# Two heads' last attention rows scored in both halves of TensorE's columns, and ten more heads scored in split precision

## The chip, the cores and the metric

The kernel runs on one core of a Trainium2 chip. The metric is the device time of one execution in microseconds (us); of several runs the median counts. TensorE (PE in the rows) multiplies matrices and loads their weights (PEld), VectorE (DVE) and ScalarE (ACT) do elementwise work and read TensorE's results, GpSimd (POOL) does elementwise work on data in SBUF, and SyncE (SP) issues the DMA transfers. One thing is particular to this program: every engine works through its own list in order, so an instruction that waits holds back all that stand behind it on its engine.

## The reference, cut to what matters

Causal attention with a decay goes through two gated feed-forward layers. Four batches, eight heads, 576 positions, head width 64:

```python
scores = scale * np.matmul(q, k.transpose(0, 1, 3, 2))
log_f = np.log(np.clip(f, 0.0001, 1.0))
cum = np.cumsum(log_f, axis=-1)
decay = cum[:, :, :, None] - cum[:, :, None, :]
scores = np.where(causal, -1000000000.0, scores + decay)
attn = np.exp(scores - np.max(scores, axis=-1, keepdims=True))
attn = attn / (np.sum(attn, axis=-1, keepdims=True) + 1e-09)
attn_out = np.matmul(attn, v)
...
x = (x @ w_a) * (x @ w_b) @ w_out          # 2304 x 512, then 1536, then 512
...
g = rmsnorm(x) @ w_gate                     # the second layer, the same sizes
out = silu(g) * (rmsnorm(x) @ w_val) @ w_out2
```

## The kernel before, in words

The 2304 tokens are worked through in three chunks (640, 704 and 1024 wide), and each chunk goes through both layers in six phases. The products of the layers are made of a high and a low part of each operand: a `triple` is three matmuls (lines 903, 904, 905) in the type fp32r. These matmuls are nearly all of TensorE's work. The weights arrive as 64-bit numbers and are decoded in the first phase: the last step, on GpSimd, is the low part at line 764.

Attention is cut into jobs that are woven between the blocks of the layers. The list `ATT` says which: a batch, its blocks of 128 query rows (`ALL` is 0 to 128, 128 to 256, 256 to 384, 384 to 512 and the last one, 512 to 576, with 64 rows), and a number `sf`. Group 0 has the later rows of batch 0, group 1 batch 1 and the first 128 rows of batch 2, group 2 the rest of batch 2, group 3 batch 3. Heads are taken two at a time. A head below `sf` has its scores in plain fp32: one matmul of 66 contracted rows, which the trace shows as two records. The other heads are split: GpSimd copies (line 1890) and VectorE subtractions (line 1893) make high and low parts in `qa`, `ka` and `b` from the loaded `qk`, and a score is then two fp32r matmuls, one of 128 contracted rows from `qa` and `ka`, one of 68 from `b`. There is one buffer each of `qk` and `b`, and two each of `qa` and `ka`, which is one pair of heads.

`unit` (line 1922) scores one block of 128 rows of one head against all keys up to it. `packed` (line 1948) scores the last 64 rows of both heads of a pair in one tile of 128 partitions, in two column halves of 288 keys, each in an own bank `s` (there are two). It does so by first writing all 128 partitions with head 1, whose 128 query columns end at the last row, and then the lower 64 with head 0. After the softmax the probabilities are transposed (line 1565, fp32), copied out, and multiplied with the values (`values`, line 1978): fp32 matmuls with 64 weight columns, the two heads of a pair in turn, one to each half of the output's partitions. Where a group of other rows is light enough, the last 64 rows share this job with it, and stand ahead of it.

The order on each engine is made in advance by `Plan`: it knows a cost of every step and a priority, places the steps greedily, tries nine ways of weighing them for every stretch of 30 us, and writes the order out. A changed cost or an added step therefore moves instructions all over the program. `kind` marks TensorE steps in fp32, and a change from fp32 to fp32r counts 85 ns there.

Of the kernel before, what the change touches and what calls it, by code (L numbers as in the profile page):

```python
# [28 lines left out]
ALL = tuple((a, min(a + 128, S)) for a in range(0, S, 128))  # L29
FIRST = ((0, 128), (128, 256))  # L30
PE, ACT, DVE, POOL, SP = "PE", "ACT", "DVE", "POOL", "SP"
# [15 lines left out]

ATT = [
    (((0, ((256, 384), (384, 512), (512, 576)), 8),), ((0, 0.0, 0.22, 1.0),), 18000),
    (((1, ALL, 2), (2, ALL[:1], 8)), ((0, 0.22, 0.8, 1.0),), 5000),  # L50
    (((2, ALL[1:], 0),), ((1, 0.1, 1.0, 0.6), (2, 0.0, 0.2, 0.4)), 5000),
    (((3, ALL, 0),), ((2, 0.1, 1.0, 0.7), (3, 0.1, 0.88, 0.3)), 20000),
]
# [27 lines left out]
def mm(n):  # L81

    return max(107.0, 0.4375 * n + 7)


def values_cost(nkb, n):

    return nkb * 2 * (2 * n / 2.4 + 6) + 210
# [86 lines left out]
class Plan:  # L175
# [19 lines left out]
    def op(self, eng, cost, fn, reads=(), writes=(), prio=0.0, after=(), nbytes=0, start=0, port=False, kind=0):  # L195
        n = Node()
        n.port, n.kind = port, kind
        n.eng, n.cost, n.fn, n.prio, n.bytes, n.ready = eng, cost, fn, prio, nbytes, start
        deps, n.allocs, n.bufs, n.first = set(after), [], set(), set()
        for t in (*reads, *writes):  # L200
            b = t[0] if isinstance(t, tuple) and isinstance(t[0], Buf) else t
            if isinstance(b, Buf):
                if b.alloc is None:
                    b.alloc = n
                    n.allocs.append(b)
                    self.rings.setdefault(b.tag, []).append(b)
                elif b.alloc is not n:
                    n.first.add(b.alloc)
                if b not in n.bufs:
                    n.bufs.add(b)  # L210
                    b.users.append(n)
        for t in reads:
            assert t in self.writer, t
            deps.add(self.writer[t])
            self.readers.setdefault(t, []).append(n)
        for t in writes:
            if t in self.writer:
                deps.add(self.writer[t])
            deps.update(self.readers.get(t, ()))
            self.writer[t] = n  # L220
            self.readers[t] = []
        deps.discard(n)
        n.first -= deps
        deps |= n.first
        n.deps, n.outs, n.waiting = deps, [], len(deps)
        for d in deps:
            d.outs.append(n)
        n.given, n.att = (eng, cost, fn, start), False
        self.nodes.append(n)
        return n  # L230
# [153 lines left out]
class Kernel:  # L384
# [219 lines left out]
    def blocks(self, p):  # L604

        m, c = PHASES[p]
        n = range(len(CHUNKS[c][1]))
        if c == 0:
            if p:
                return [x for q in range(THIRDS) for x in self.plain_blocks(q, n)]  # L610
            ab = lambda fs, ss: [("ab", j, s) for f in fs for j in (2 * f, 2 * f + 1) for s in ss]
            y = lambda q, ss: [("y", i, q, s) for i in range(KT) for s in ss]
            cut = QF + ALONE
            return [
                *self.plain_blocks(0, [0]), *ab(range(QF, cut), [0]), *ab(range(cut, 2 * QF), n),
                *ab(range(QF, cut), [1]), *y(1, n), *self.plain_blocks(2, n), *self.plain_blocks(0, [1]),
            ]
        ahead = int(self.adjoins(p))
        out = [*((x, f) for f in range(2) for x in ("P1", "P2")), ("P7", 0)] if ahead else [("P1", 0), ("P7", 0), ("P2", 0)]
        for f in range(FT):  # L620
            out += [("P6", f), ("P4", f)]
            nxt = [[(x, f + 1)] if f + 1 < FT and (x == "P7" or f >= ahead) else [] for x in ("P1", "P7", "P2")]
            out += [*nxt[0], ("P5", f), *nxt[1], *nxt[2], ("P3", f)]
            if f == FT - 1 or (p < SWAP_AT and f % QF == QF - 1):
                out += [("y", i, f // QF, s) for i in range(KT) for s in n]
            elif p >= SWAP_AT and f and f % QF == FAST_AFTER:
                out += [("z", i, f // QF - 1, k) for k in range(len(FAST)) for i in range(KT // 2)]
        if self.adjoins(p + 1):
            out[-2 * KT :] = [("y", i, THIRDS - 1, s) for s in n for i in range(KT)]
        return out  # L630
# [1302 lines left out]
    def packed(self, c, u, tiles, t, sf):  # L1933

        nc, op = self.nc, self.op
        a, e = u
        r, w = e - a, e // 2
        assert 2 * r == 128
        s = [self.bank("s", S_BANKS) for _ in range(2)]
        qk = [x for y in tiles for x in y[1]]  # L1940
        for i in range(2):

            def scores(x, ks=slice(i * w, i * w + w)):

                for g in (1, 0):
                    n, y = g * r + r, tiles[g][0]
                    for j, (q, k) in enumerate(y):
                        nc.tensor.matmul(x[:n, :w], q.tile[:, e - n : e], k.tile[:, ks], start=j == 0, stop=j == len(y) - 1)  # L1948

            op(PE, 2 * (4 * w / 2.4 + 3 if sf else 2 * mm(w)), scores, reads=qk, writes=[s[i]], prio=t, kind=int(sf))  # L1950
        p = self.tile([128, S], "P", P_BUFS, pool=self.att)
        sm = self.tile([128, 2], "sm", 4, pool=self.att)
        self.exps(128, e, [self.mask[:, 0:w], self.mask_2], s, p, sm, 0, t + 600)
        self.norms(128, e, [p], sm, 2, t + 600)
        return p, None

    def values(self, c, hs, groups, tiles, t):

        nc, op = self.nc, self.op
        some = [self.moved(us, pss, t) for us, pss in groups]  # L1960
        reads = [x for r, _ in some for x in r]
        starts, width = [], 0
        for us, _ in groups:
            starts.append(width)
            width += us[-1][1] - us[0][0]
        blocks = lambda u: -(-u[1] // 128)
        rows = lambda u, i: min(128, u[1] - i * 128)
        pv = self.bank("tp", TP_BANKS)

        def product(x):  # L1970
            for (us, _), (_, at), start in zip(groups, some, starts):
                for j, u in enumerate(us):
                    o, n = start + u[0] - us[0][0], u[1] - u[0]
                    for i in range(blocks(u)):
                        k = rows(u, i)
                        for g in range(2):
                            y, to = at[g, j, i]
                            nc.tensor.matmul(  # L1978
                                x[64 * g : 64 * g + 64, o : o + n], tiles[g][2][0].tile[:k, i, :], y.tile[:k, to : to + n],
                                start=i == 0, stop=i == blocks(u) - 1,  # L1980
                            )

        op(
            PE, sum(values_cost(blocks(u), u[1] - u[0]) - 210 for us, _ in groups for u in us) + 210, product,
            reads=[*reads, *(x for y in tiles for x in y[2][1])], writes=[pv], prio=t + 5500, kind=1,
        )
        for (us, _), start in zip(groups, starts):
            self.valued(c, hs, us[0][0], us[-1][1], start, pv, t)
# [127 lines left out]
```

## Time and profile before

| what | us |
|---|---|
| median of 3 runs | 1075.48 |
| lowest and highest of them | 1072.12, 1080.87 |
| the profiled execution's own time | 1073.34 |
| its span, first to last instruction | 1071.3 |
| TensorE busy in it | 1050.6 |
| VectorE busy | 807.7 |
| ScalarE busy | 565.1 |
| GpSimd busy | 249.2 |

The time outside of the span is 2.0 us. A matmul's record covers its whole way through the array, and the next one starts before it ends; what one costs in a row of many is the distance from start to start. The chain of waits gives this distance, since it counts each piece up to where the next takes over.

### The profile page before, as it was taken

Reading aid. Unit: us, or ns where it says so; the run is one execution under the profiler, and the core shown is the slowest. Engines: PE = TensorE matmul, PEld = TensorE weight load, DVE = VectorE, ACT = ScalarE, POOL = GpSimd, SP = SyncE. Lnnn points to the kernel's source line nnn. Section 1 sums busy time; section 2 is a strip of 40 time slices with the busy share of each in tenths; the row PEclk is TensorE's granted clock in tenths of the full one; section 3 lists DMA queues with packets and bytes.
Section 4 is the critical chain, followed back from the end, with each engine's and each line's share of the span. In section 5 each row is a group of like instructions: output and inputs, shape, how many; then the busy total and the mean of one; then the engine's idle time right before and its main releaser. Section 6 shows DMA issues by size and latency. Waiting matters only on the chain.

```text
span 1071.3 us, 19068 instructions
## 1 busy us (share of the span) xinstructions
PE 1050.6 (98%) x6738; PEld 934.5 (87%) x6738; DVE 807.7 (75%) x1815; ACT 565.1 (53%) x1235; POOL 249.2 (23%) x254
## 2 busy tenths in 40 slices
PE   8999999999999999999999999999999999999998
PEld 6678889999999999999999999988888887788886
DVE  6787677779668877878779777765667469979974
ACT  6677578656444557665665663522333254444330
POOL 6423244312203134443541010000000023212000
PEclk9999999999999999999999999999999999999999
DMA  8989868989865986678789676786453634546332
GB/s 232 270 267 305 311 201 276 311 303 340 265 214 207 323 284 230 223 234 290 267 311 332 225 258 234 256 282 195 143 171 120 206 117 151 171 140 180 120 124 78
DMA packets 91707, 245.54 MB, mean 229 GB/s; under 512 B 13077, under 2 KB 23525, under 8 KB 91613
## 3 DMA queue, kind: packets, MB, share of 16 engines
q1 hardware_dynamic: 91612, 244.33, 68.7%
q8 instruction: 53, 0.87, 0.3%
q14 instruction: 42, 0.34, 0.1%
HBM read 163.27 MB, written 81.03 MB: 228 GB/s over the span
## 4 chain that ended last, share of the span: by engine, by line
PE 82%; DVE 8%; DMA 3%; issue 3%; POOL 2%; ACT 1%; SPq 0%; DVEq 0%; POOLq 0%; ACTq 0%
PE m L903 19%; PE m L905 18%; PE m L904 18%; PE tp L1978 4%; PE tp L1565 3%; PE s L1922 3%; PE s L904 2%; PE s L905 2%; PE s L903 2%; PE tp L904 2%; PE tp L905 2%; PE tp L903 2%; PE s L1948 2%; POOL w L764 1%; DMA w<-wd 1%
## 5 line engine op out<-in xcount | busy, mean ns | idle before, releaser
L903 PE MATMUL m<-E,w 128*128 128x512 f32 (+3 forms) x672 | 234.1, 348 | 4.9 <-ACT a L1291 1.7
L905 PE MATMUL m<-E,w 128*128 128x512 f32 (+3 forms) x672 | 227.4, 338 | 0.6 <-POOL w L764 0.6
L904 PE MATMUL m<-E,w 128*128 128x512 f32 (+3 forms) x624 | 212.7, 341 | 0.0
L1291 ACT ACTIVATE a<-m 128x352 f32<-128x352 f32 (+1 forms) x144 | 74.9, 526 | 146.6 <-PE m L905 146.1
L764 POOL TENSOR_TENSOR w<-w,w 128x512 fp32r<-128x512 f32 x72 | 98.4, 1372 | 201.9 <-ACT w L1614 149.9
L903 PEld LDWEIGHTS m<-E,w 128*128 128x128 f32 x672 | 126.7, 189 | 21.3 <-issue 3.7
L904 PE MATMUL m<-Eb,w 128*128 128x352 f32 (+3 forms) x432 | 140.9, 326 | 0.0
L905 PEld LDWEIGHTS m<-E,w 128*128 128x128 f32 x672 | 126.4, 188 | 11.4 <-POOL w L764 0.8
L1300 DVE TENSOR_TENSOR a<-m,a 128x352 f32<-128x352 f32 (+1 forms) x144 | 86.5, 602 | 58.6 <-PE m L905 57.7
L903 PE MATMUL m<-Eb,w 128*128 128x352 f32 (+3 forms) x384 | 127.5, 332 | 0.1
L904 PEld LDWEIGHTS m<-E,w 128*128 128x128 f32 x624 | 117.6, 189 | 11.1 <-issue 0.2
L905 PE MATMUL m<-Eb,w 128*128 128x352 f32 (+3 forms) x384 | 126.8, 330 | 0.0
L903 PE MATMUL m<-G,w 128*128 128x352 f32 (+2 forms) x352 | 111.0, 315 | 0.4 <-DVE xc L941 0.3
L905 PE MATMUL m<-G,w 128*128 128x352 f32 (+2 forms) x352 | 108.3, 308 | 0.2 <-POOL w L764 0.2
L904 PE MATMUL m<-G,w 128*128 128x352 f32 (+2 forms) x352 | 108.2, 307 | 0.0
L1524 ACT ACTIVATE P<-P,mn 128x512 f32<-128x512 f32 (+4 forms) x128 | 76.1, 596 | 23.6 <-DVE mn L1517 22.9
L904 PEld LDWEIGHTS m<-Eb,w 128*128 128x128 f32 x432 | 81.3, 188 | 4.3
L903 PEld LDWEIGHTS m<-Eb,w 128*128 128x128 f32 x384 | 72.2, 188 | 4.9 <-DVE a L1300 0.4
L905 PEld LDWEIGHTS m<-Eb,w 128*128 128x128 f32 x384 | 72.2, 188 | 4.3
L1427 ACT ACTIVATE G<-a 128x352 fp32r<-128x352 f32 (+3 forms) x100 | 47.1, 473 | 52.3 <-DVE a L1413 18.8
L1517 DVE CUSTOM_DVE_ANT_0 P<-s,mask 128x512 f32<-128x512 f32 (+4 forms) x128 | 61.5, 495 | 13.3 <-PE s L1922 7.0
L903 PEld LDWEIGHTS m<-G,w 128*128 128x128 f32 x352 | 66.3, 188 | 2.7 <-issue 1.2
(268 smaller groups left out, 2258.0 us busy)
## 6 DMA issues: line engine op xcount, KB each, us to landing
w<-wd SPq DMA_DIRECT2D x88, 512.0 KB
wd<-w SPq DMA_DIRECT2D x72, 512.0 KB
ws<-w SPq DMA_DIRECT2D x48, 512.0 KB
w<-ws SPq DMA_DIRECT2D x48, 512.0 KB
wf<-w SPq DMA_DIRECT2D x48, 256.0 KB
raw<-wo SPq DMA_DIRECT2D x24, 512.0 KB
w<-wf SPq DMA_DIRECT2D x48, 256.0 KB
w<-wd SPq DMA_DIRECT2D x48, 256.0 KB
```

Of the source, the lines that this page charges most:

```text
L764: nc.gpsimd.tensor_tensor(out=w.tile[:, :, 1, :], in0=i32.tile.bitcast(F32), in1=w.tile[:, :, 0, :].bitcast(F32), op=ALU.subtract)
L903: mm_(o, wh, xh, start=start, stop=False)
L904: mm_(o, wh, xl, start=False, stop=False)
L905: mm_(o, wl, xh, start=False, stop=stop)
L1291: nc.scalar.activation(z[:, :h], bank_.tile[:, :h], AF.Copy)
L1300: nc.vector.tensor_tensor(out=z, in0=bank_.tile[:, :h], in1=z, op=ALU.add)
L1427: nc.scalar.activation(out(0), x(), AF.Copy)
L1517: nc.vector.tensor_tensor_reduce(out=p.tile[:n, i * w : i * w + w], in0=s[i].tile[:n, :w], in1=masks[i][:n], scale=-0.125, scalar=mn.tile[ ...
L1524: nc.scalar.activation(o, o, AF.Exp, bias=mn.tile[:n, len(s) - 1 : len(s)], scale=-1.0, accum_out=sm.tile[:n, g : g + 1])
L1565: nc.tensor.transpose(ps.tile[:w, c : c + n], p.tile[:n, i * 128 : i * 128 + w], self.ident[:n, :n])
L1922: self.nc.tensor.matmul(x[:n, :e], q.tile[:, a:e], k.tile[:, :e], start=j == 0, stop=j == len(pairs) - 1)
L1978: nc.tensor.matmul(x[64 * g : 64 * g + 64, o : o + n], tiles[g][2][0].tile[:k, i, :], y.tile[:k, to : to + n], start=i == 0, stop=i == blo ...
```

## The change

Three things change. `ATT` asks for no fp32 scores in group 1 any more: the first two heads of batch 1 and the first rows of all eight heads of batch 2 become split. `packed` is written in two forms: for fp32 heads (batch 0 alone now) each head's 64 query columns go to their own half of the output partitions, head 0 and head 1 in turn; for split heads the two column halves of head 1 come first and then those of head 0, as four steps of the planner where there were two. `values` goes through its groups from the last to the first, so that the last 64 rows come last where they share the job.

```diff
-    (((1, ALL, 2), (2, ALL[:1], 8)), ((0, 0.22, 0.8, 1.0),), 5000),
+    (((1, ALL, 0), (2, ALL[:1], 0)), ((0, 0.22, 0.8, 1.0),), 5000),
...
-        for i in range(2):
-
-            def scores(x, ks=slice(i * w, i * w + w)):
-
-                for g in (1, 0):
-                    n, y = g * r + r, tiles[g][0]
-                    for j, (q, k) in enumerate(y):
-                        nc.tensor.matmul(x[:n, :w], q.tile[:, e - n : e], k.tile[:, ks], start=j == 0, stop=j == len(y) - 1)
-
-            op(PE, 2 * (4 * w / 2.4 + 3 if sf else 2 * mm(w)), scores, reads=qk, writes=[s[i]], prio=t, kind=int(sf))
+        pairs = [y[0] for y in tiles]
+
+        def scores(parts, *_):
+            for g, i, b, n in parts:
+                for j, (q, k) in enumerate(pairs[g]):
+                    nc.tensor.matmul(
+                        s[i].tile[b : b + n, :w], q.tile[:, e - n : e], k.tile[:, i * w : i * w + w], start=j == 0,
+                        stop=j == len(pairs[g]) - 1,
+                    )
+
+        if sf:
+            for i in range(2):
+                parts = [(g, i, g * r, r) for g in range(2)]
+                op(PE, 2.1 * w, partial(scores, parts), reads=qk, writes=[s[i]], prio=t + i, kind=1)
+        else:
+            for g in (1, 0):
+                for i in range(2):
+                    op(PE, 2 * mm(w), partial(scores, [(g, i, 0, r + g * r)]), reads=qk, writes=[s[i]], prio=t + 2 - 2 * g + i)
...
-            for (us, _), (_, at), start in zip(groups, some, starts):
+            for (us, _), (_, at), start in list(zip(groups, some, starts))[::-1]:
```

TensorE's list, the second pair of heads of batch 0, before: the packed fp32 scores (line 1948) into two banks, with the values of the pair before them (line 1978) in between.

```order
L1948 MATMUL s_726<-b_449 128x288
L1948 MATMUL s_726<-b_449 64x288
L1978 MATMUL tp_739<-pt_721,vr_434 64x64 x8
L1978 MATMUL tp_739<-pt_719,vr_434 64x64 x2
L1948 MATMUL s_758<-b_449 128x288
L1948 MATMUL s_758<-b_449 64x288
L1565 MATMUL tp_766<-ident,P_664 128x128 x3
```

And now (the packed scores are at line 1946, the values at line 1986):

```order
L1922 MATMUL s_706<-b_366 128x512
L1986 MATMUL tp_715<-pt_700,vr_434 64x64 x8
L1986 MATMUL tp_715<-pt_703,vr_434 64x64 x2
L1946 MATMUL s_738<-b_449 64x288 x2
L1946 MATMUL s_744<-b_449 64x288 x2
L903 MATMUL m_758<-E,w_678 128x256
```

No packed fp32 matmul has 128 output partitions any more, and the two banks follow each other.

TensorE's list, one values job of batch 1 in which the last 64 rows (output 64x64) share the tile with a block of 128 rows, before:

```order
L905 MATMUL m_2120<-G,w_2075 128x256
L1978 MATMUL tp_2143<-pt_2088,vr_1882 64x64 x8
L1978 MATMUL tp_2143<-pt_2091,vr_1882 64x64 x2
L1978 MATMUL tp_2143<-pt_2118,vr_1882 64x128
L1978 MATMUL tp_2143<-pt_2133,vr_1882 64x128
```

And the end of the same kind of job now:

```order
L1986 MATMUL tp_2183<-pt_2172,vr_1914 64x128
L1986 MATMUL tp_2183<-pt_2177,vr_1914 64x128
L1986 MATMUL tp_2183<-pt_2105,vr_1914 64x64 x8
L1986 MATMUL tp_2183<-pt_2119,vr_1914 64x64 x2
L1922 MATMUL s_2218<-ka_1912,qa_1863 128x512
```

The two rows of `x2`, whose matmuls contract over 64 positions, moved from the middle of the job to its end.

GpSimd's list, from the late part of group 0 on, before: the low parts of decoded weights (line 764) and between them the split copies of one pair of batch 1 (line 1890).

```order
L764 TENSOR_TENSOR w_1672<-w_1648,w_1672 128x2x256
L764 TENSOR_TENSOR w_1742<-w_1721,w_1742 128x2x256
L1890 TENSOR_SCALAR b_1771<-qk_599 64x576 x2
L764 TENSOR_TENSOR w_1838<-w_1797,w_1838 128x2x256
L764 TENSOR_TENSOR w_1891<-w_1853,w_1891 128x2x256
L764 TENSOR_TENSOR w_2075<-w_2045,w_2075 128x2x256
L1890 TENSOR_SCALAR qa_2135<-qk_1949 64x576
L1890 TENSOR_SCALAR ka_2141<-qk_1949 64x576
```

And now, over the same part of batch 1's first two pairs:

```order
L764 TENSOR_TENSOR w_1561<-w_1523,w_1561 128x2x256
L1890 TENSOR_SCALAR qa_1603<-qk_962 64x128
L1890 TENSOR_SCALAR ka_1605<-qk_962 64x128 x2
L1890 TENSOR_SCALAR qa_1624<-qk_962 64x128
L1890 TENSOR_SCALAR b_1622<-qk_962 64x128 x2
L1890 TENSOR_SCALAR ka_1629<-qk_962 64x128 x2
L1430 TENSOR_TENSOR G<-a_1538,G 128x256
L764 TENSOR_TENSOR w_1649<-w_1597,w_1649 128x2x256
L764 TENSOR_TENSOR w_1700<-w_1673,w_1700 128x2x256
L764 TENSOR_TENSOR w_1789<-w_1745,w_1789 128x2x256
L1890 TENSOR_SCALAR qa_1841<-qk_1725 64x576
L1890 TENSOR_SCALAR qa_1863<-qk_1725 64x576
```

A set of eight short copies for the first rows of batch 2 now stands between those of two pairs of batch 1, with weight parts behind it.

## Rows read from the trace of the kernel before

**Rows 1.** The page: busy time by engine, and TensorE's clock over 40 slices.

```profile
PE 1050.6 (98%) x6738; PEld 934.5 (87%) x6738; DVE 807.7 (75%) x1815; ACT 565.1 (53%) x1235; POOL 249.2 (23%) x254
...
PEclk9999999999999999999999999999999999999999
```

**Rows 2.** What TensorE waited for: total us, times, longest us.

```profile
PE tp L1565 <- ACT P L1548: 2.3, 4, 1.1
...
PE m L903 <- ACT a L1291: 1.7, 2, 1.0
...
PE m L905 <- POOL w L764: 0.8, 2, 0.6
```

**Rows 3.** Busy time by stretch: length, then each engine's.

```profile
core 0: us, PE busy (x) PEld busy (x) DVE busy (x) ACT busy (x) POOL busy (x), PEclk, DMA share, GB/s
30.00:105.00 75.00, 74.67 (x571) 54.88 (x570) 57.01 (x174) 56.04 (x135) 24.06 (x22) 1.00 0.90 280
105.00:215.00 110.00, 105.93 (x879) 99.22 (x879) 81.43 (x223) 77.82 (x199) 43.40 (x43) 1.00 0.83 275
215.00:620.00 405.00, 400.20 (x3025) 386.27 (x3025) 318.52 (x815) 238.57 (x563) 118.87 (x129) 1.00 0.79 269
```

**Rows 4.** The chain that ended last, in time order: start, us, work, records.

```profile
45.00 1.29 PE s L1922 x4
...
49.17 0.87 PE tp L1565 x8
50.05 1.72 PE s L1922 x4
51.77 1.68 PE tp L1978 x28
...
54.03 2.43 PE s L1948 x8
...
308.30 0.71 PE s L1922 x4
...
400.06 0.93 PE s L1922 x4
...
530.50 1.08 PE s L1948 x8
```

**Rows 5.** TensorE's timeline, three short windows of one values job from 176.75 us.

```profile
176.75 0.63 PE L1978 MATMUL tp<-pt,vr 128*64 128x64 f32 x14
...
177.36 0.33 PE L1978 MATMUL tp<-pt,vr 64*64 64x64 f32 x4
...
177.62 0.33 PE L1978 MATMUL tp<-pt,vr 128*64 128x128 f32 x2
```

**Rows 6.** Groups by shape, the split's copies and subtractions: busy us, mean ns, idle before.

```profile
L1890 POOL TENSOR_SCALAR b<-qk 64x576 fp32r<-64x576 f32 x14 | 10.2, 744 | 3.3 <-PE s L1922 3.3
...
L1890 POOL TENSOR_SCALAR b<-qk 64x448 fp32r<-64x448 f32 x8 | 4.4, 558 | 8.3 <-PE s L1922 8.3
...
L1893 DVE TENSOR_TENSOR qa<-qk,qa 64x576 fp32r<-64x576 f32 x14 | 13.2, 956 | 0.4
...
L1893 DVE TENSOR_TENSOR qa<-qk,qa 64x448 fp32r<-64x448 f32 x8 | 5.3, 683 | 0.2
```

**Rows 7.** What GpSimd waited for: total us, times, longest us.

```profile
POOL w L764 <- ACT w L1614: 149.9, 37, 12.7
...
POOL qa L1890 <- PE s L1922: 23.7, 8, 6.9
```

## The prediction

> **What bounds the kernel now.** The page comes first: TensorE is busy for 1050.6 us of a span of 1071.3, at full clock in all 40 slices [rows 1]. Busy time alone doesn't prove it the bound, since records overlap, so the waits come next. The longest kinds of wait of TensorE are a few us each: 2.3 us for ScalarE's probabilities, 1.7 for an evacuation, 0.8 for a weight part from GpSimd [rows 2]. So nearly the whole span is matmuls that follow each other without a gap, and a microsecond of TensorE work that vanishes should be a microsecond of time, as long as no other engine falls behind. The stretches tell where one could. From 30 to 105 us, where batch 0's fp32 scores are, TensorE is idle for 0.33 of 75 us; from 105 to 215 us, where group 1 of the attention lies, for 4.07 of 110, with VectorE at 81.43 and GpSimd at 43.40 us [rows 3]. That second stretch is the only one of the three in which TensorE is hungry, and it is where the change adds work for the other two.
>
> What a score costs is read from the chain of waits, since there each piece ends where the next begins [rows 4]. Two heads of fp32 scores cost 1.29 us for 384 keys and 1.72 for 512; split, 0.71 and 0.93. The packed fp32 job of a pair costs 2.43 us, the split one 1.08.
>
> **The change, part by part.**
>
> *Packed fp32 scores of batch 0, four pairs.* Eight records of 288 keys, at the pace of the unpacked rows (1.29 us / 4 records for 384 keys, so 0.24 each for 288), would be 1.93 us. The job takes 2.43, so half a microsecond of it goes where the output changes from 128 to 64 partitions and back. The new form has only 64-column weights, one head in each half. No row shows scores in that form; the nearest is the values job, which is also fp32, with 64 weight columns and the two heads in turn. Its 28 records of 128 columns take 1.68 us, 60 ns each, where 8 transposes of 128 columns take 0.87 us, 109 ns each [rows 4]. So two halves run at once and a record costs 0.55 of a lone one. 1.93 x 0.55 = 1.06, with a little for entry 1.1 us. The gain is 2.43 - 1.1 = 1.33 a pair, 5.3 us for four. The bounds: if the halves don't overlap at all, 1.93 stands and 2.0 us are gained; if they overlap wholly and nothing is lost at the entry, 0.97 stands and 5.8 are gained. I take 5.3, since the values job is the same form in all but the moving operand.
>
> The Trainium skill has a rule against this, in "TensorE: Matmul & The Clock Gate", section "The mechanism": a weight load overlaps running matmuls only when it goes to another group of rows. The two heads here use the same rows and differ in columns alone, so by that rule the gain would be the 2.0 us. The values rows disagree with it at 60 against 109 ns.
>
> *First two heads of batch 1, from fp32 to split.* For the pair: 512 keys 1.72 - 0.93 = 0.79; 384 keys 1.29 - 0.71 = 0.58; 256 keys in proportion to 384, 0.86 - 0.47 = 0.39; 128 keys next to nothing, 0.1; packed 2.43 - 1.08 = 1.35 [rows 4]. Together 3.2 us, all on TensorE's path.
>
> *First rows of batch 2, eight heads, from fp32 to split.* By proportion to 512 keys a pair would go from 0.43 to 0.23 us, but the transposes show that a matmul of 128 columns costs 0.11 however cheap its type, and four of them are 0.44 [rows 4]. Between 0 and 0.2 a pair I take 0.1, 0.4 us for four.
>
> *Values from the last group to the first.* In the job at 176.75 us the sixteen records of 64 columns before 177.36 take 0.61 us, 0.038 each. The four records that contract over 64 rows only take 0.26, up to 177.62, where 0.15 would do [rows 5]: 0.11 us go into the change back to 128 rows. At the end of the job the next work pays for a change of shape in any case, so the change in the middle vanishes. Twelve jobs share a tile like this (four pairs each of batches 1 to 3): 1.3 us, and with the slower first records after 177.62 a little more; I take 1.5, between 0 (if the end of the job now costs that much more) and 1.9.
>
> *Packed split scores in four steps.* The matmuls are the same ones, and the split job shows 1.08 / 8 = 0.135 us a matmul, which is what 384 keys give in proportion (0.71 / 4 x 288 / 384 = 0.133). So no change of shape is paid here before, and none is saved. The first bank is complete two matmuls later, 0.27 us, and VectorE starts on it by that much later; TensorE has layer blocks in between. Nothing.
>
> *What is added on GpSimd, VectorE and SyncE.* By the order GpSimd gets eight more copies of 576 columns and 32 of 128 columns. The first cost 0.74 us each, 5.9 us. For 128 columns there is no row; between 0.16 (448 columns in proportion, 0.558 x 128 / 448) and 0.56 I take 0.25, nearer to the proportional end because 448 and 576 columns differ by 0.19: 8 us [rows 6]. 14 us in all, where 43.4 of 110 are busy. VectorE gets four subtractions of 576 columns at 0.96 and sixteen of 128, between 0.2 and 0.68, at 0.27: 8 us, to some 89 of then about 105. On SyncE the loads go to `qk` where they went to `b`, as many and as large; costed at nothing. GpSimd's copies hide behind layer blocks as long as its list doesn't hold the weight parts up; what stands behind the copies there is line 764, and TensorE waits for that in line 905 [rows 2].
>
> *What is given back.* The work above lands in the hungry stretch. From nothing to a doubling of its 4.07 us of idle [rows 3], I take 2.5.
>
> The sum: 5.3 + 3.2 + 0.4 + 1.5 = 10.4, less 2.5, is 7.9 us. The profiled execution took 1073.34 us, so 1065.4; it lies 2.1 us under the median of 1075.48, and against that the forecast is **1067.5 us**. A measurement of this kernel can tell about 1% (10.8 us) from no change, so the forecast sits inside of that.
>
> **The rivals.**
>
> *Nothing is given back.* The planner knows the new costs, reorders all engines, and TensorE has fewer changes between fp32 and fp32r in its list (207 for 215). At 0.15 us each, the size of the changes of shape above, that is 1.2 us more: 11.6 us, 1063.9. For it speaks that TensorE's waits are small everywhere and that the planner can move probabilities and evacuations from VectorE to ScalarE, which has 32 us free in the hungry stretch [rows 3]. Against it: a reordering of the whole list makes new small waits somewhere.
>
> *The halves don't overlap, or most of the gain is lost in reordering.* The packed job gains 2.0 instead of 5.3: 10.4 - 3.3 - 2.5 = 4.6, 1070.9. The 288 keys are longer than any moving operand of the values rows, and both heads read different keys; for the overlap speak 28 records at 60 ns.
>
> *GpSimd's gate: slower.* The first copy of each pair waits until TensorE has finished the scores of the pair before, since `qa` and `ka` have room for one pair. GpSimd lost 23.7 us in 8 such waits, 3.0 each [rows 7]. In group 1 three pairs were split; now eight are, five gates more. If each gate with its copies (3.0 + 8 x 0.25 = 5.0 us) delays the weight part behind it and TensorE with it, 25 us are lost and 10.4 gained: 1090. It decides from the point where a gate is longer than GpSimd's lead: line 764 waited 149.9 us in 37 pieces for ScalarE, 4 us a piece [rows 7], so delays under 4 us vanish. That speaks against it.
>
> **How the numbers follow.** The forecast, 1065 to 1069, gets 0.48; nothing given back 0.24; no overlap or lost in reordering 0.2; the gate 0.08. Faster by over 1% means under 1064.7: all but a little of the first rival, and some of the forecast's lower edge with the spread of a median, 0.35. Slower by over 1% is the gate, 0.07. The rest, 0.58, is within 1%. The range leaves out the gate and the outermost tenth on the fast side: from 1061 (the first rival less the 3 us by which runs scatter about their median) to 1077 (all gains lost, and a little).
>
> **What the profile of the changed kernel would show.** Packed fp32 jobs of 1.0 to 1.2 us in the chain of waits, with records of the two heads that start within some ns of each other; no score records of 66 rows after 100 us; values jobs whose records of 64 rows come last. In the stretch of group 1 GpSimd would be busy for some 14 us more, and VectorE for some 8. TensorE's waits would be a few us longer in total there. The prediction is wrong if the packed job stays near 2 us, if line 905 waits for line 764 by more than some us, or if the stretches after 215 us, which have the same work but for eight values jobs, differ in length by more than 3 us.

## The result: about 0.7% slower, and the profile after

| | before | after |
|---|---|---|
| median of 11 runs each | 1072.6 us | 1082.32 us |
| lowest to highest | 1069.54 to 1080.87 | 1075.51 to 1087.72 |
| profiled execution, span | 1073.34, 1071.3 | 1087.72, 1085.9 |

The ratio after/before is 1.0073 [1.0049, 1.0097]. The forecast was 7.9 us of gain; what came is some 8 us of loss, above the upper end of the range (1077.0). It is still within the 1% that was called no change. The profiled execution is the longest of the eleven, which matters below: what its rows show of the clock is more than a usual run lost.

The page of after (busy time by engine, TensorE's clock in 40 slices, shares of the chain that ended last) answers to [rows 1]:

```profile
PE 1054.8 (97%) x6738; PEld 940.9 (87%) x6738; DVE 822.3 (76%) x1827; ACT 567.1 (52%) x1240; POOL 268.5 (25%) x297
...
PEclk8889999999999999999999999999999999999999
...
PE 77%; DVE 12%; DMA 5%; ACT 3%; issue 2%; POOL 1%; SPq 0%; DVEq 0%; ACTq 0%; POOLq 0%
```

The same three stretches as in [rows 3], in after:

```profile
core 0: us, PE busy (x) PEld busy (x) DVE busy (x) ACT busy (x) POOL busy (x), PEclk, DMA share, GB/s
30.00:105.00 75.00, 70.74 (x546) 54.64 (x542) 52.23 (x149) 51.20 (x119) 23.78 (x22) 0.89 0.78 247
105.00:215.00 110.00, 103.80 (x852) 96.11 (x852) 88.30 (x249) 75.12 (x203) 55.14 (x71) 1.00 0.80 273
215.00:620.00 405.00, 396.56 (x3009) 382.21 (x3007) 324.33 (x816) 241.84 (x566) 127.10 (x143) 1.00 0.80 273
```

TensorE's idle time grew in all three: 0.33 to 4.26 us, 4.07 to 6.20, 4.80 to 8.44. In the first the granted clock is 0.89, where it was 1.00. In finer steps, the same view of after:

```profile
0.00:25.00 25.00, 21.65 (x124) 17.95 (x124) 16.26 (x63) 16.81 (x47) 13.62 (x23) 0.86 0.80 224
25.00:45.00 20.00, 18.21 (x132) 12.96 (x131) 11.08 (x40) 10.64 (x30) 10.94 (x15) 0.91 0.74 215
45.00:65.00 20.00, 16.86 (x122) 12.06 (x121) 17.17 (x46) 14.51 (x34) 6.79 (x6) 0.89 0.86 253
65.00:85.00 20.00, 20.00 (x135) 15.13 (x135) 13.68 (x41) 12.24 (x29) 3.60 (x3) 0.76 0.63 217
```

The worst stretch for the clock, 65 to 85 us, has TensorE busy throughout; it comes behind the stretch with the most idle time. TensorE's timeline shows what stands between (start, length, form, records, and in brackets the idle time before and who ended it):

```profile
43.17 1.19 PE L1946 MATMUL s<-b 66*64 66x288 f32 x8
...
47.59 0.55 PE L1565 MATMUL tp<-ident,P 128*128 128x128 f32 x3 [0.32 <-ACT P L1548]
48.62 0.55 PE L1565 MATMUL tp<-ident,P 128*128 128x128 f32 x3 [0.48 <-DVE P L1550]
49.76 1.37 PE L1922 MATMUL s<-b 66*128 66x512 f32 x2 [0.59 <-DVE mn L1517]
...
62.31 0.30 PE L1565 MATMUL tp<-ident,P 128*64 128x128 f32 x1 [1.76 <-DVE E L2070]
```

The waits of TensorE, total us, times, longest, answer to [rows 2]. None is long, but new ones stand there, nearly all for VectorE:

```profile
PE s L1922 <- DVE mn L1517: 3.2, 5, 1.4
...
PE tp L1565 <- DVE E L2070: 1.8, 1, 1.8
PE s L1922 <- DVE x L941: 1.5, 1, 1.5
...
PE m L905 <- POOL w L764: 1.3, 2, 0.7
...
PE s L1946 <- DVE b L1893: 1.3, 1, 1.3
...
PE s L1922 <- DVE b L1893: 0.7, 1, 0.7
```

The chain in order of time answers to [rows 4]:

```profile
67.70 1.71 PE s L1922 x2
...
79.65 1.12 PE s L1946 x8
...
140.28 1.06 PE s L1946 x8
```

The packed fp32 job costs 1.12 us, where the forecast had 1.1. The row at 67.70 is one head's 512 keys in two records; that is what both heads cost in [rows 4], 1.72 in four records. It lies in the stretch in which the clock is at its half level.

**Where the time went.** Each record's time up to the start of the next, summed by kind, splits TensorE's time from its first record to its last, 1066.0 us before and 1080.8 after, without remainder (idle time goes to the record ahead of it):

| us | before | after |
|---|---|---|
| packed scores | 27.59 | 22.91 |
| scores of single blocks | 46.51 | 55.33 |
| values | 52.63 | 49.88 |
| transposes | 41.38 | 47.45 |
| the layers' matmuls | 859.98 | 864.32 |
| the start and the norms | 37.92 | 40.90 |

Packed scores and values are shorter, as forecast. Everything else is longer, most of all the single blocks' scores, whose matmuls the change was to make cheaper. Of their 55.33 us 6.66 are idle time, of the 46.51 before 0.57; and the stretch at half clock falls on them.

**The clock's part.** At half clock the same work takes twice as long (the row at 67.70 above), so a stretch of length L with a mean clock of c loses L(1 - c). These four rows give 3.5 + 1.8 + 2.2 + 4.8 = 12.3 us; before lost 1.8 us, in its first 25. This profile is an extreme: of the eleven runs, all of one program, the one with a clock of 0.999 took 1075.51 us and the one with 0.988 took 1087.72, and the others lie between in nearly that order (0.995 is the median clock). 0.011 x 1086 = 11.9 us, against 12.2 measured. So the spread of after's runs is the clock, and even the run that lost almost nothing to it is 2.9 us slower than before's median. Before's profiled run has 0.998: at the median clock 3.2 us of the loss are clock, at the 0.994 of the run with the median time 4.3. That is a third to a half; the rest is waits, which have also eaten the gain of the scores.

### The profile page after: what moved, and what is told of

Same layout as the page of the kernel before. It is cut to its first block, busy times and chain, and to the rows that moved or that the text cites. A ratio compares the mean times of both kernels' runs of the same rounds, so it can differ in the third digit from the quotient of the medians.

```text
span 1085.9 us, 19142 instructions
## 1 busy us (share of the span) xinstructions
PE 1054.8 (97%) x6738; PEld 940.9 (87%) x6738; DVE 822.3 (76%) x1827; ACT 567.1 (52%) x1240; POOL 268.5 (25%) x297
## 4 chain that ended last, share of the span: by engine, by line
PE 77%; DVE 12%; DMA 5%; ACT 3%; issue 2%; POOL 1%; SPq 0%; DVEq 0%; ACTq 0%; POOLq 0%
PE m L903 18%; PE m L905 17%; PE m L904 17%; PE s L1922 3%; PE tp L1986 3%; PE tp L1565 3%; PE s L904 2%; PE s L905 2%; PE s L903 2%; PE tp L904 2%; PE tp L905 2%; PE tp L903 2%; DVE w L756 2%; DMA raw<-wv 1%; DVE qa L1893 1%
```

## The experiments

Three theories were tried. Theory 1: the single gains are real, and the loss comes from the new order on all engines and the half clock behind it. Theory 2: the loss is GpSimd's and VectorE's work for the ten heads that are split now (2a the eight short ones of batch 2, 2b the two long ones of batch 1). Theory 3: batch 0's softmax sets the pace of its stretch, and what TensorE saves is waited out. Where nothing else is said, times are medians, and ratios are against the kernel before on the same chip (its median 1074.42, 1073.07 and 1073.12 us in the three series).

### The parts by themselves

**e2_halves**: the kernel before, with the packed fp32 scores in halves, at the old costs and in two steps.

```diff
-                for g in (1, 0):
-                    n, y = g * r + r, tiles[g][0]
+                for g in (0, 1) if sf else (1, 0):
+                    n, o, y = (r, g * r, tiles[g][0]) if sf else (g * r + r, 0, tiles[g][0])
...
-                        nc.tensor.matmul(x[:n, :w], ...)
+                        nc.tensor.matmul(x[o : o + n, :w], ...)
```

> The packed fp32 scores go to both halves of the columns, with the old costs told to the planner, so that every engine keeps the order of before (here ten packed jobs' halves, five pairs, since the first pair of batch 1 stays fp32). Theory 1 (the order: the single gains are real, the loss of the whole change comes from the new order of all engines, in which TensorE waits for VectorE in the first 65 us and then runs at half clock for a while): 5 x 1.33 = 6.6 us faster, ratio 0.994, packed jobs of 1.1 us, clock as before. Theory 2 (the extra split heads load VectorE and GpSimd): the same 6.6 us. Theory 3 (batch 0's softmax decides, and what TensorE saves in its scores it waits out): within 2 us of before, with 5 us more of TensorE's idle between 30 and 105 us, and stretches at half clock there.

Measured: 1070.46 us, 0.9961 [0.9944, 0.9977]. Summed from start to start, the packed scores (five fp32 pairs here, with batch 1's) fall from 27.59 to 20.64 us, 1.39 a pair. About 4 of these 7 us arrive by the medians (2.5 to 6.0 by the interval); the two profiled runs, both at a clock of 0.998, differ by 5.5.

**e5_halves_values**: that, and the values from the last group to the first.

```diff
-            for (us, _), (_, at), start in zip(groups, some, starts):
+            for (us, _), (_, at), start in list(zip(groups, some, starts))[::-1]:
```

> As the kernel with the halves alone, and the values from the last group to the first; the order of all engines stays that of before. Theories 1 and 2: 6.6 + 1.5 = 8.1 us faster, ratio 0.9925. Theory 3: the values' 1.5 us alone, since they lie mostly after batch 0, ratio 0.998.

Measured: 1071.14 us, 0.9972 [0.9954, 0.9989]. The values take 49.45 us for e2's 51.18, so 1.7 us are saved on TensorE. Nothing of it is seen in the time, but the two ratios, with intervals of 0.17% each, could not tell 1.7 us from nothing.

**e3_split**: the kernel before, with the new row of `ATT` alone.

```diff
-    (((1, ALL, 2), (2, ALL[:1], 8)), ((0, 0.22, 0.8, 1.0),), 5000),
+    (((1, ALL, 0), (2, ALL[:1], 0)), ((0, 0.22, 0.8, 1.0),), 5000),
```

> The kernel before with the table of heads alone changed: no fp32 scores in batch 1 and in the first rows of batch 2. All engines get a new order. By its TensorE work it would gain 3.2 + 0.4 = 3.6 us. Theory 2: all of the loss is here, 9.7 + 5.3 + 1.5 = 16 us slower than before, ratio 1.015, with TensorE's waits in the stretch of batch 1 from 105 to 215 us. Theory 1: a new order, so that the sign is open, but TensorE's idle and the half clock decide it and not VectorE's load: within 6 us of before, and the gain of 3.6 us plus the growth of idle and of half clock accounts for the span. Theory 3: 3.6 us faster, ratio 0.997, since batch 0 keeps its slow scores.

Measured: 1086.67 us, 1.0118 [1.0097, 1.0139]. The part to which the forecast gave 3.6 us of gain loses 12.7. Its clock is 0.997 in the profiled run, and TensorE's idle time is 27.4 us for 15.8, so this loss is nearly all waits. The longest kind is for ScalarE's probabilities (2.3 us in [rows 2]), which got none of the work itself; the next lines are for GpSimd's weight part and VectorE's subtractions, the engines that got it (TensorE's waits in e3):

```profile
PE tp L1565 <- ACT P L1548: 5.7, 5, 3.6
PE m L905 <- POOL w L764: 3.3, 3, 1.5
...
PE s L1948 <- DVE b L1893: 1.6, 2, 1.0
...
PE s L1922 <- DVE b L1893: 1.2, 2, 0.6
```

**e4_no_split**: the changed kernel with the old row of `ATT` (e3's edit backwards).

> The changed kernel with the old table of heads: halves, values turned round, split packed scores in four steps, but no more split heads than before. All engines get a new order. By its TensorE work it would gain 6.6 + 1.5 = 8.1 us. Theory 2: it does gain them, ratio 0.9925. Theory 1: open in sign, and the gain of 8.1 us minus the growth of TensorE's idle and of time at half clock accounts for the span; if waits before 65 us and a half clock show as in the changed kernel, it is slower than the kernel with halves and values in the old order by those. Theory 3: no faster than before, ratio 1.0, with idle and half clock between 30 and 105 us.

Measured: 1075.0 us, 1.0007 [0.9992, 1.0023]. It has the same savings as e5 and, besides, the packed split scores in four steps, the new costs and thereby another order; that takes back e5's 3 us, 3.8 by the ratios. From e4 to after, by their ratios, the split adds 0.66%, 7 us, in an order that is another one again. This puts the greater part of the loss on the split and leaves theory 1 some 4 us.

### Which heads, and which planner steps

**e6_b1** and **e7_b2**: e5 with one half of the new row each; **e8_all_old_cost**: e5 with both, so that it differs from after only in the two planner steps and old costs of the packed scores.

```diff
+    (((1, ALL, 0), (2, ALL[:1], 8)), ...    # e6_b1
+    (((1, ALL, 2), (2, ALL[:1], 0)), ...    # e7_b2
+    (((1, ALL, 0), (2, ALL[:1], 0)), ...    # e8_all_old_cost
```

> Halves and values in the old form of the planner's steps and costs, and the first two heads of batch 1 split; the first rows of batch 2 stay fp32. The planner makes a new order. On TensorE's path it gains 1.9 us over halves and values alone (the packed job of that pair is in halves already). Theory 2a (the eight short heads are the harm): 1069, as halves and values alone or 2 us better. Theory 2b (the long heads, with 6 us of copies on GpSimd): most of the 12 us of the split alone, 1080. Theory 1 (any new order costs): 3 to 6 us slower than halves and values in the old order, 1075.

> Halves and values in the old steps and costs, and the first rows of batch 2's eight heads split; the first two heads of batch 1 stay fp32. New order. Theory 2a: 10 us and more slower than halves and values alone, 1081 or more, with TensorE waiting in the scores of 128 keys and in line 905 for line 764. Theory 2b: within 3 us of halves and values alone, 1071. Theory 1: 1075.

> All of the change but the four steps of the packed split scores and the planner's new cost of the packed fp32 ones: the split, the halves and the values. New order, another one than the changed kernel's. Theory 2 (the split as such): as slow as the changed kernel or the split alone less 7 us for halves and values, 1079 to 1083. Theory 1 (which order comes out decides): anywhere between 1068 and 1085.

Measured: e6 1077.67 us, 1.0044 [1.0026, 1.0063]; e7 1086.77, 1.0125 [1.0098, 1.0153]; e8 1085.69, 1.0109 [1.0083, 1.0135]. Against e5's 0.9972 the two long heads cost 0.72%, 7.7 us, the eight short ones 1.53%, 16 us, and both together 1.37%, no more than the short ones alone. So in these orders, one of each kind, the short heads are the worse part, though their 8 scores were to gain 0.4 us. And the old steps and costs make the loss larger, not smaller: the four steps of the packed split scores are not its cause.

### The added work alone, in an unchanged order

Each of these kernels still has an order of its own. The next four have e5's order on every engine, instruction for instruction, and only have work put in that nobody reads: GpSimd copies and VectorE subtractions of 64x128, issued with the scores of the heads in question, into one scratch tile.

```diff
+    def scratch(self, copies, rests):
+        x = self.att.tile([128, n], F32, tag="sc", bufs=1, name=f"sc{self.nsc}")
...
+        for i in range(copies):
+            nc.gpsimd.tensor_scalar(
+                out=x[0:64], in0=self.mask[0:64, :n], scalar1=1.0, scalar2=0.0, op0=ALU.mult, op1=ALU.add
+            )
+        for i in range(rests):
+            nc.vector.tensor_tensor(out=x[64:128], in0=self.mask[64:128, :n], in1=self.mask[64:128, :n], op=ALU.subtract)
...
+                if a == 0 and (c == 2 or (c == 1 and sf)):
+                    self.scratch(4, 2) if c == 2 else self.scratch(9, 5)
```

**e9_load** is this as it stands, 50 copies and 26 subtractions. **e10_load_pool** has the copies only, **e11_load_dve** the subtractions only. **e13_load_late** has both at the first scores of batch 3 (`if a == 0 and c == 3`), far behind batch 0.

> Halves and values in the old order of all engines, and beside it the load of the split without its use: with the first score of each head that the change splits, GpSimd makes 4 copies of 64 x 128 (9 for the two heads of batch 1) and VectorE 2 (5) subtractions into a scratch tile that nobody reads. This work is added to the kernel's own. If the load alone is the harm (the copies hold up line 764, the subtractions the softmax): 8 us or more slower than halves and values alone, 1079 and up. If it is the dependence (each pair's split waits for the scores of the pair before and TensorE for the split) or the new order: within 3 us, 1072 to 1074.

> Halves and values in the old order, with the scratch copies of GpSimd alone (50 of 64 x 128, some 15 us), beside the kernel's own work; VectorE gets nothing more. If GpSimd's list is the harm (copies ahead of the weight parts of line 764): 1080 or more, as with both loads. If VectorE's list is: 1071 to 1074. If the two share it, for example since a copy on GpSimd makes VectorE's own work longer: between, 1076 to 1079, with longer times of VectorE's line 756 in the stretch from 87 to 215 us.

> Halves and values in the old order, with the scratch subtractions of VectorE alone (26 of 64 x 128, some 8 us), in front of the maxima of the scores. If VectorE's list is the harm (the softmax of each pair comes later by them, and TensorE waits for a bank or for probabilities): 1079 or more. If GpSimd's is: 1071 to 1074.

> Halves and values in the old order, with the same 50 copies and 26 subtractions as with both loads, but at the first scores of batch 3's heads, after 215 us, where weights come ready from DRAM and GpSimd is busy for a third of the time. If the place decides (in the first phase the decoding of the weights fills GpSimd, ScalarE and VectorE): within 4 us of halves and values alone, 1071 to 1075. If such a load costs its length anywhere: 1079 and up.

Measured: e9 1086.05 us, 1.0118 [1.0094, 1.0142]; e10 1082.98, 1.0085 [1.0064, 1.0106]; e11 1081.85, 1.0075 [1.0055, 1.0095]; e13 1081.07, 1.0067 [1.0048, 1.0086]. Against e5 that is 15.7, 12, 11 and 10 us. What was put in, by e10 and e11 (count, busy us, mean ns, idle before):

```profile
L1918 POOL TENSOR_SCALAR sc<-mask 64x128 f32<-64x128 f32 x50 | 22.1, 442 | 3.8
L1918 DVE TENSOR_TENSOR sc<-mask 64x128 f32<-64x128 f32 x26 | 9.8, 378 | 0.8
```

A copy takes 0.29 us where nothing lengthens it, but the 50 keep GpSimd busy for 22.1 us, and the 26 subtractions VectorE for 9.8. So of GpSimd's added time, on an engine that is a quarter busy, 12 of 22 us come out as time of the kernel, and of VectorE's all of it. With the order unchanged, theory 1's order can't be the reason of these losses. Nor is it that the copies slow VectorE down: its own instructions take 3.7 us more in e10 than in e5, of 903 us summed. How it comes about is read in e10, GpSimd and TensorE on one timeline:

```profile
93.97 7.46 POOL L1918 TENSOR_SCALAR sc<-mask 64x128 f32<-64x128 f32 x15
...
101.40 2.49 POOL L764 TENSOR_TENSOR w<-w,w 128x512 fp32r<-128x512 f32 x2
...
102.71 0.58 PE L905 MATMUL m<-E,w 128*128 128x256 f32 x1 [3.61 <-POOL w L764]
```

The weight part stands behind the copies in GpSimd's list, and TensorE stands waiting for it. In e11 five subtractions at a time stand ahead of the softmax's maxima, and TensorE waits for the bank that these free:

```profile
92.79 1.58 DVE L1918 TENSOR_TENSOR sc<-mask 64x128 f32<-64x128 f32 x5
...
94.47 0.27 DVE L1517 CUSTOM_DVE_ANT_0 P<-s,mask 128x128 f32<-128x128 f32 x1
...
94.80 0.70 PE L1933 MATMUL s<-b 66*128 66x256 f32 x2 [1.86 <-DVE mn L1517]
```

The totals of these waits, e5, e10 and e11 (TensorE's waits):

```profile
PE m L905 <- POOL w L764: 1.4, 2, 0.7
PE s L1922 <- DVE mn L1517: 1.4, 5, 0.4
```

```profile
PE m L905 <- POOL w L764: 7.5, 4, 3.6
...
PE s L1961 <- POOL w L764: 2.3, 1, 2.3
```

```profile
PE tp L1565 <- ACT P L1548: 5.7, 3, 2.7
PE s L1933 <- DVE mn L1517: 4.0, 7, 1.9
```

And behind the idle places the clock falls. The stretch 87 to 130 us of e5, e10 and e11:

```profile
87.00:130.00 43.00, 41.22 (x343) 36.78 (x342) 29.12 (x86) 28.01 (x71) 12.53 (x11) 1.00 0.91 317
```

```profile
87.00:130.00 43.00, 36.89 (x280) 31.59 (x279) 25.85 (x76) 24.66 (x63) 21.47 (x35) 0.88 0.76 259
```

```profile
87.00:130.00 43.00, 37.58 (x283) 32.74 (x280) 31.28 (x91) 24.31 (x62) 11.93 (x10) 0.88 0.79 269
```

e10's idle time grew there by 41.22 - 36.89 = 4.3 us, and its clock takes 0.12 x 43 = 5.2 us more. e11's figures are 3.6 and 5.2. Since instruction follows instruction in the same order, the delay can be followed from e5 to each of them: TensorE is 1.8 us ahead at 85 us in e10 (e5's profiled run has a clock of 0.89 in its first 30 us, e10's 0.94) and 6.7 behind at 106, 12.6 at 197, and 12.5 at the end. Nothing is caught up afterwards. The two together (e9) cost less than their sum, 16 for 23, presumably as both stop TensorE in part at the same time.

e13 says that such work costs behind batch 0 too, though a third less than in e9: its load lies from 433 to 601 us; TensorE is some 3 us ahead of e5 up to 215 us and 1.5 at 257, then 4.2 behind at 555 and 10.6 at 599, with one wait of 4.9 us in a layer block (line 903, for VectorE, which has two runs of seven subtractions ahead of line 1300 there) and a clock of 0.996. Its last two bursts, 13 copies and 7 subtractions each, are larger than any of e9's (9 and 5), and more than 6 us are lost at them.

Three reservations. In e9 and e13 both engines write one scratch tile, so they also wait for each other there, 6.1 and 9.9 us in all; e10 and e11 have only one writer, no such wait, and carry the argument. The load is heavier than the split's own work, 22.1 us on GpSimd where lines 1890 take 16.1 more in after than before, and 9.8 on VectorE for 7.9 at lines 1893, and it comes in bursts that no plan has spread; so its prices are rather upper bounds for after, where the planner knew of the work. And no score waits for the load, so what the split costs because a score waits for it is not in these prices; TensorE's waits for line 1893 are 2.0 us in after, 2.8 in e3 and 0.2 before. That after loses 7 us to the split, and e6 to e8 in another order 7.7 to 16, says that the planner hides some of it at best.

**e12_act_copies**: the changed kernel with the 32 short copies on ScalarE, which is half idle; the planner makes a new order.

```diff
+        by, cost = (ACT, act) if k1 == 128 else (POOL, pool1)
...
-        op(POOL, pool1(n), lambda x: copy(x[0:64, q0:k1], qr()[:, q0:k1]), ...
+        op(by, cost(n), lambda x: copy(x[0:64, q0:k1], qr()[:, q0:k1]), ...
```

> The changed kernel with the 32 short copies of batch 2's first rows on ScalarE, which is idle for 35 of the 110 us from 105 to 215; the order is new once more. If GpSimd's copies are what costs: 8 us or more faster than the changed kernel, 1074 or less. If it is VectorE's subtractions or the dependence of each pair on the scores before: within 4 us of the changed kernel, 1079 to 1086.

Measured: 1087.57 us, 1.0123 [1.0103, 1.0143], slower than after. In this order taking the copies off GpSimd doesn't help; TensorE's idle time is 31.3 us (after 26.4, before 15.8, all as gaps between records). Whether that is ScalarE, which delivers the probabilities, or the new order was not separated. A version that keeps the split and wins was not found; the best kernels of this study are e2 and e5, at 0.996 and 0.997 of before.

## Why the prediction was wrong

**What held.** The packed fp32 job: 1.12 us measured for 1.1. The Trainium skill ("TensorE: Matmul & The Clock Gate", "The mechanism") says that a weight load overlaps running matmuls only when it goes to another group of rows. Read as the prediction read it, this would make the job cost 1.93 us, and the row at 79.65 contradicts that reading: heads that differ in columns alone overlap with scores of 288 keys as well. The values: 1.7 us of TensorE's list for the forecast 1.5 (e5 against e2). The packed split job at 1.06 us beside 1.08: nothing gained or lost by the four steps. Two of the prediction's signs of being wrong, a packed job near 2 us and a long wait of line 905 for line 764 (1.3 us), did not show. The size of the added work held too (busy us, mean ns, idle before), after's answer to [rows 6]:

```profile
L1890 POOL TENSOR_SCALAR ka<-qk 64x128 fp32r<-64x128 f32 x16 | 5.5, 342 | 1.1
L1890 POOL TENSOR_SCALAR qa<-qk 64x128 fp32r<-64x128 f32 x8 | 2.4, 302 | 4.4 <-PE s L1922 4.3
L1890 POOL TENSOR_SCALAR b<-qk 64x128 fp32r<-64x128 f32 x8 | 2.3, 302 | 0.0
...
L1893 DVE TENSOR_TENSOR qa<-qk,qa 64x128 fp32r<-64x128 f32 x8 | 2.5, 314 | 0.3
L1893 DVE TENSOR_TENSOR b<-qk,ka 64x128 fp32r<-64x128 f32 x8 | 2.1, 286 | 0.1
```

10.2 us for 8 on GpSimd, 4.6 for 4.3 on VectorE; in the stretch from 105 to 215 us GpSimd is busy for 11.7 us more (14 forecast) and VectorE for 6.9 (8 forecast).

**What failed** is the step "What is given back", 2.5 us, and with it the cover that "What is added" claimed for the copies behind the layer blocks. Between the 10.4 us of single gains and the 8 us of loss some 18 us were given back. By the ratios they fall into three parts: e5 got 3 of the 8.1 us that its halves (five pairs) and values were to gain, so 5 are missing before any order changes; the way from e5 to e4, with a new order, costs 4; and from e4 to after the split costs 7 net, 9 with the 2.3 us that it was still to gain there (e4 has one of its pairs in halves already). In the kernel before (e3) the split costs 12.7 net, 16 with its 3.6. The bound was taken from the idle time of one stretch, doubled at most. In that stretch it nearly held: from 105 to 215 us TensorE's idle time grew by 2.1 us. But it grew by 3.9 from 30 to 105 us and by 3.6 from 215 to 620, where the step looked for nothing.

Two things were missed. Added work does not just fill GpSimd's free time, it delays what stands behind it in the list, and the lists of GpSimd, VectorE and ScalarE run close enough ahead of TensorE that 9.8 us more on VectorE, or 22.1 on GpSimd, cost 11 or 12 (e11, e10). And an idle place of TensorE may bring a stretch at half clock behind it, a term that the prediction didn't have at all. It read full clock off the page's nines [rows 1], but a nine is 90% or more of a slice of 27 us, and the 0.998 of that run was 1.8 us lost in the first 25.

A smaller term had the wrong sign. The first rows of batch 2 were to gain 0.4 us on TensorE. Start to start, with idle time left out, a score of 128 keys takes 0.21 us as two fp32 records in the trace of before, and 0.23 there as two split matmuls, 0.26 in after. So the eight short heads lose 0.4 us on TensorE too.

**The first two claims about the bound.** "A microsecond of TensorE work that vanishes should be a microsecond of time, as long as no other engine falls behind": e2 got about 4 of 7 us, and e5 3 of 8.1. Theory 3 holds for a small part of this: from 30 to 105 us TensorE's idle time is 2.2 us in e2 where it was 0.33, not 5 more, and from 105 to 215 us it is 2.9 where it was 4.07. The rest was not traced. The hungry stretch was the place looked at, but after's profiled run lost most of its time ahead of it: in the first 85 us half clock took 10.5 us more than before and idle time 3.3 more. Where the other runs, with less half clock, lost theirs is not on record.

**The rivals.** "Nothing is given back" (1063.9) had the wrong sign. "The halves don't overlap, or most of the gain is lost in reordering" (1070.9) is wrong in its first half, and its second falls short, as more than the whole gain was lost. "GpSimd's gate" (1090, chance 0.08) had the sign and nearly the size of e3 and e8, and its place, line 764 ahead of line 905, shows in e3 with 3.3 us. But it was a rival about one engine; VectorE alone does as much (e11), and in after line 905 waits for 1.3 us only (0.8 in [rows 2]). Its reason against itself, that delays under 4 us vanish because line 764 waits 4 us a piece for ScalarE [rows 7], was a mean over the whole span and said nothing of the stretch of the copies.

**Of the theories**, 2 is the best borne out: that work of this kind costs 11 to 12 us without any new order is shown (e10 and e11, less cleanly e9 and e13); that it is what the split costs in after is argued from that and from e3, e4 and e7, each in an order of its own. 2a weighs more than 2b in the one order of each. Theory 1's order has some 4 us (e4 against e5), its clock a third to a half of after's loss in a median run. What stays open: which of the new waits in after's first 65 us stem from which part. From 45 to 65 us TensorE is idle for 3.1 us in after, 0.5 in e4 and 1.1 in e8, but for 2.9 in e6 and 3.5 in e12, and no run separated them. Whether work put into TensorE's idle places would keep the clock up was not tried.

## What to carry to other kernels

When every engine runs a written-out list close behind the next, an engine's free share is no cover: ask of each added instruction what stands behind it in that list and by how much TensorE is ahead there, and price it at half to all of its length until shown otherwise (12 of 22 us on GpSimd here, 11 for 10 on VectorE). An unread load in an unchanged order measures that price before any plan is redone; read from the trace how long the load itself came out. Trading TensorE time for many short instructions elsewhere (here a forecast 0.4 us, which the records don't show, for 48 of 0.3 us each) is the trade to distrust first.

## What the runs showed of the hardware

Two streams of fp32 scores with 64 weight columns each, 288 keys long and on the same rows, run side by side: 1.12 us for eight records where the form with 128 and 64 columns took 2.43 [rows 4].

The granted clock fell to its half level behind short idle places of TensorE: after a stretch with 16.86 of 20 us busy it was 0.76 over the next 20 us, which were busy throughout; e10 shows the same behind a wait of 3.6 us, with 0.88 over 43 us. It does not fall behind every such place: in e11 TensorE is busy for 16.8 of 20 us from 150 to 170 us, and the clock is 1.00 there and in the next 45 us. The price goes by (1 - clock) x span, 12.2 us between 0.988 and 0.999 over runs of one program.

In after a 64x128 copy on GpSimd takes 0.30 to 0.34 us in the mean of its groups and a 64x128 subtraction on VectorE 0.29 to 0.31, where the copy of 576 columns takes 0.74 and the subtraction 0.96 [rows 6]: 4.5 times fewer columns cost about 2.3 and 3.2 times less.

How long a copy on GpSimd takes went with what VectorE did beside it. Of e10's 50 equal copies the fastest took 0.29 us, among them those that ran beside VectorE's line 1517 alone; the 13 slowest, 0.64 to 0.88 us, all ran beside VectorE's lines 752, 756 or 1893. Three of these are among the 15 that fill 7.46 us in the row at 93.97.
